# The last block's routing in a transformer-and-experts kernel: merged VectorE operations, and four weight splits postponed

## The chip, the cores and the metric

One NeuronCore of one Trainium2 chip runs the whole program. The metric is the device time of one execution in microseconds. The kernel before took 767.72, 769.78 and 770.45 us in three runs; the median is 769.78 us.

## The reference, cut to what matters

Three stages run one after the other on 2304 tokens (4 sequences of 576) of width 512, all in float32:

```
attn   = softmax(mask(q k^T / 8)) v           # 8 heads of 64, causal window of 64
h      = x @ w_in                             # 512 -> 2048
x1     = (max(h,0) + alpha*min(h,0)) @ w_out  # 2048 -> 512
logits = x1 @ w_gate                          # 8 experts
e      = argmax(logits);  p = softmax(logits)[e]
out    = p * (max(x1 @ w1[e], 0) @ w2[e])     # 512 -> 1024 -> 512, each token by its one expert
```

What the change touches is the third stage: the routing, that is which token goes to which expert, and the order in which the experts' weights are prepared.

## The kernel before, in words

**Blocks.** The 18 token tiles of 128 are cut into five blocks of 4, 4, 4, 3 and 3 tiles. Attention and the dense stage run block by block under a written-out plan, the last block (index 4, called L in the code) from line 1014 on in a loop that the framework schedules. Products are made from a high and a low part of each operand: three TensorE matmuls (hi*hi, hi*lo, lo*hi) for one exact one.

**Slots.** The expert stage works in slots: a slot is up to 128 tokens of one expert. It gathers its tokens' rows of x1 from DRAM (`gather`), transposes them (`xtr`), multiplies by w1 in four parts (`e1`), transposes the result (`htr`), multiplies by w2 in four parts (`e2mm`) and scatters the rows to the output (`finish`). Slots 0 to 7 use tokens of the first four blocks only; their table (which expert and which list column a slot has) is built in the last dense block. The other slots need the last block's routing, which is done while slots 3 to 6 run. 21 slots run with these inputs (0 to 20); slots 20 to 24 stand under a branch.

**Weights.** A slot's weights are eight pieces of 128x1024. ScalarE writes each piece's high part (`split2_hi`, line 937) and VectorE its low part (`split2_lo`, line 943) into a ring of 12 tiles. SyncE reloads the raw piece pair for a later slot behind each second split, if that slot has another expert. In `slot(s)` there are eight steps, one behind each part of the matmul work; in the kernel before step i of slot s splits piece i of slot s+1, so a piece is ready a whole slot before it is used.

**Routing of the last block.** Its logits are made in slots 0 to 2. Then two chains of small VectorE operations, `route_main` (argmax, ranks, list) and `route_side` (softmax weight, slot table), are fed in by `tick(n)`, which advances the first chain that is not held by n operations; behind each split stand up to two. HOLD makes a chain wait for the next `safe()` point. `r_rank` counts on TensorE how many earlier tokens chose each expert; `r_place` turns ranks to list positions; `r_onehot` and `r_list` write the token list `lst` by matmul; `slot_table` makes the slots' experts (`ctl`), change flags and list columns (`col`). `table_count` copies the totals by one more matmul into a bank of PSUM, out of three banks in rotation (`pbank("att")`) that `htr` and `xtr` use as well, and `ni` (line 649) reads it.

Of the kernel before, what the change touches and what calls it, by code (L numbers as in the profile page):

```python
# [21 lines left out]
LO_POOL = ()  # L22
# [58 lines left out]
def attn_moe_moe_kernel(  # L81
# [73 lines left out]
    def prep_consts():  # L155
        DVE.memset(lst, BIG)
        DVE.memset(ohsum, 0.0)
# [322 lines left out]
    def r_pick(j):  # L480
# [23 lines left out]
        yield  # L504
# [42 lines left out]
    def r_place(j):  # L547
# [8 lines left out]
        DVE.tensor_tensor(out=rr, in0=rk, in1=oh, op=ALU.mult)  # L556
        give(("R", j))
        yield
        for u in range(n):
            DVE.tensor_tensor(out=ohsum, in0=ohsum, in1=oh[:, u, :], op=ALU.add)  # L560
            yield
# [5 lines left out]
        yield  # L567
        ri = small("ri", [], I32)
        DVE.tensor_copy(out=ri, in_=rf)
# [10 lines left out]
        jf = small("jf", [])  # L580
        DVE.tensor_copy(out=jf, in_=ji)
        yield
        cf = small("cf", [])
        DVE.tensor_scalar(out=cf, in0=mx, scalar1=-float(NTILE), scalar2=float(NE * NTILE), op0=ALU.mult, op1=ALU.add)
        yield
        DVE.tensor_tensor(out=cf, in0=cf, in1=jf, op=ALU.add)
        yield
        rc[j] = (cf, pf)

    def r_onehot(j, h=0):  # L590
# [3 lines left out]
        for t in range(2 * h, min(2 * h + 2, n)):  # L594
            a = rp.tile([128, NCOL], FP32R, tag="A", bufs=2, name="A")
            bm = rp.tile([128, 128], FP32R, tag="B", bufs=2, name="B")
# [4 lines left out]
            yield  # L601
            ab[j].append((t, a, bm))
# [30 lines left out]
    def table_count(part=1):  # L633
        b = pbank("att") if part else aslot(("R", NB))
        PE.matmul(out=b[:, 0:NE], lhsT=one16, rhs=ohsum, start=True, stop=True)
        return b

    def slot_table(part):
        ns, s0 = (K1, 0) if part == 0 else (NSLOT - K1, K1)

        def small(nm, shape, dt=FP32):
            n = {"cmp": ns * NE, "es": ns, "jn": ns}.get(nm)
            pad = {} if n is None else {"padded_shape": [128, NSLOT] if len(shape) == 1 else [128, NSLOT, NE]}
            own = nm if nm in ("ni", "t8", "cmp", "es", "jn") else f"{nm}{part}"
            return e2.tile([128] + shape, dt, bufs=1, tag=own, name=nm, **pad)

        b = counted[0] if part else table_count(0)
        ni = small("ni", [NE], I32)
        DVE.tensor_scalar(out=ni, in0=b[:, 0:NE], scalar1=127.0 * part, scalar2=None, op0=ALU.add)
        yield  # L650
# [3 lines left out]
        DVE.tensor_copy(out=nb, in_=ni)  # L654
        yield
        give(("R", NB))
        if part:
            DVE.tensor_tensor(out=nb, in0=nb, in1=tab["done"], op=ALU.subtract)
            yield
# [3 lines left out]
        cum = small("cum", [NE])  # L663
        DVE.tensor_reduce(out=cum, in_=t8, axis=AX.X, op=ALU.add)
# [8 lines left out]
        ec = small("ec", [ns])  # L673
        DVE.tensor_scalar(out=ec, in0=es, scalar1=float(NE - 1), scalar2=None, op0=ALU.min)
        yield
        ctl = small("ctl", [2, ns], I32)
        DVE.tensor_copy(out=ctl[:, 0, :], in_=ec)
        yield
        DVE.tensor_tensor(out=ctl[:, 1, 1:ns], in0=ec[:, 1:ns], in1=ec[:, 0:ns - 1], op=ALU.not_equal)
        yield  # L680
        if part:
            DVE.tensor_tensor(out=ctl[:, 1, 0:1], in0=ec[:, 0:1], in1=tab["last"], op=ALU.not_equal)
            yield
            tot = small("tot", [1], I32)
# [9 lines left out]
        DVE.tensor_tensor(out=jn, in0=siota[:, 0:ns], in1=jn, op=ALU.subtract)  # L694
        yield
        col = small("col", [ns])
        DVE.scalar_tensor_tensor(out=col, in0=es, scalar=float(NTILE), in1=jn, op0=ALU.mult, op1=ALU.add)
        yield
        if part:
            DVE.tensor_tensor(out=cmp, in0=es.unsqueeze(2).to_broadcast([128, ns, NE]),  # L700
                              in1=siota[:, 0:NE].unsqueeze(1).to_broadcast([128, ns, NE]), op=ALU.is_equal)
            yield
            DVE.tensor_tensor(out=cmp, in0=cmp, in1=tab["done"].unsqueeze(1).to_broadcast([128, ns, NE]), op=ALU.mult)
            yield
            DVE.tensor_reduce(out=jn, in_=cmp, axis=AX.X, op=ALU.add)
            yield
            DVE.tensor_tensor(out=col, in0=col, in1=jn, op=ALU.add)
            yield
        else:
            done = small("done", [NE])  # L710
            DVE.tensor_tensor(out=done, in0=nb, in1=cum, op=ALU.subtract)
            yield
            DVE.tensor_scalar(out=done, in0=done, scalar1=float(K1), scalar2=0.0, op0=ALU.add, op1=ALU.max)
            yield
            DVE.tensor_tensor(out=done, in0=done, in1=nb, op=ALU.min)
            yield
            tab["done"] = done
# [10 lines left out]
    def route_main():  # L728
# [272 lines left out]
    at(last + 9, 6, lambda: drain(slot_table(0)))  # L1001
    at(last + 9, 6, sregs, 0)
# [25 lines left out]

    def slot(s):
# [147 lines left out]
```

## Time and profile before

| what | value |
| --- | --- |
| runs | 767.72, 769.78, 770.45 us |
| profiled execution, its own time | 767.73 us |
| its span, first to last instruction | 766.0 us |
| TensorE (PE) busy | 747.6 us, 98% |
| VectorE (DVE) busy | 607.0 us, 79% |
| ScalarE (ACT) busy | 455.4 us, 59% |
| mean granted TensorE clock | 0.996 |

The span is the time between the first and the last instruction; the execution's own time is 1.73 us more. Shares of busy time are averages over stages with different limits, so the expert stage is read slot by slot. A slot begins with its first matmul of line 833. Those starts are at 528.42 us for slot 3, 541.07 for slot 4, 558.92 for slot 5, 572.14 for slot 6, 585.85 for slot 7 and 598.16 for slot 8; from there on a slot follows every 12.3 us.

### The profile page before, as it was taken

The numbers are of one execution on the slowest core, as the hardware profiler recorded it, in microseconds if no ns is written. First come the engines' busy times: TensorE is split into PE (matmuls) and PEld (weight loads), VectorE is DVE, ScalarE is ACT, GpSimd is POOL, SyncE is SP. The second block draws the span as 40 slices with busy tenths as digits, with TensorE's granted clock in tenths as the row PEclk, the third lists the DMA queues.
The fourth block names the chain that finished last, engine by engine and source line by source line (L and its number), as shares of the span: only waits on it lengthen the run. The fifth ranks groups of instructions, "written<-read, shape, count | busy, mean of one in ns | idle before, by whom it ended". The sixth has DMA issues, their size and how long they took to land.

```text
span 766.0 us, 12642 instructions
## 1 busy us (share of the span) xinstructions
PE 747.6 (98%) x4572; PEld 612.7 (80%) x4572; DVE 607.0 (79%) x1149; ACT 455.4 (59%) x865; POOL 86.3 (11%) x106
## 2 busy tenths in 40 slices
PE   7999999999999999999999999999899999999996
PEld 3688888888888888888888988788677888888884
DVE  4999998477565756578875946689989999999997
ACT  4877555543233342334343224788678898899986
POOL 1210001000000000000000001021111213131322
PEclk9999999999999999999999999999999999999999
DMA  9983413133122222222223117411216776767611
GB/s 344 411 367 131 175 66 118 49 104 104 47 72 97 62 83 77 73 87 99 84 66 111 56 43 298 169 43 42 70 31 245 276 272 262 286 223 258 212 75 51
DMA packets 29442, 109.90 MB, mean 143 GB/s; under 512 B 3582, under 2 KB 3966, under 8 KB 22208
## 3 DMA queue, kind: packets, MB, share of 16 engines
q1 hardware_dynamic: 25856, 98.25, 35.6%
q0 software_dynamic: 3520, 10.80, 4.3%
q8 instruction: 38, 0.62, 0.3%
q14 instruction: 28, 0.23, 0.1%
HBM read 154.09 MB, written 10.26 MB: 215 GB/s over the span
## 4 chain that ended last, share of the span: by engine, by line
PE 90%; DVE 5%; DMA 2%; ACT 1%; issue 1%; SPq 0%; DVEq 0%; ACTq 0%
PE acc L861 14%; PE h L385 9%; PE acc L427 9%; PE h L386 8%; PE h L387 8%; PE acc L428 8%; PE acc L429 8%; PE h L835 4%; PE h L833 4%; PE h L834 4%; DVE hl L943 3%; PE att L360 3%; PE att L291 2%; PE att L337 2%; PE att L844 1%
## 5 line engine op out<-in xcount | busy, mean ns | idle before, releaser
L943 DVE TENSOR_TENSOR hl<-hl,hl 128x1024 fp32r<-128x1024 f32 x176 | 212.0, 1222 | 19.4 <-ACT hl L937 18.7
L937 ACT CAST hl<-hl 128x1024 fp32r<-128x1024 f32 x176 | 180.6, 1050 | 5.1 <-DMA hl<-in_wx_dram 4.0
L861 PE MATMUL acc<-hl,xl 128*128 128x512 f32 x504 | 132.4, 404 | 1.2 <-DVE xl L848 1.2
L400 ACT ACTIVATE g<-h 128x512 f32<-128x512 f32 (+1 forms) x80 | 44.6, 558 | 142.3 <-PE h L387 112.0
L385 PE MATMUL h<-xh,hl 128*128 128x512 f32 (+1 forms) x320 | 120.7, 377 | 0.6 <-DVE g L404 0.6
L386 PE MATMUL h<-xl,hl 128*128 128x512 f32 (+1 forms) x320 | 118.2, 369 | 0.0
L387 PE MATMUL h<-xh,hl 128*128 128x512 f32 (+1 forms) x320 | 118.1, 369 | 0.0
L428 PE MATMUL acc<-hl,gl 128*128 128x512 f32 x288 | 113.1, 393 | 0.3 <-DVE gl L410 0.3
L429 PE MATMUL acc<-hl,gh 128*128 128x512 f32 x288 | 112.7, 391 | 0.0
L427 PE MATMUL acc<-hl,gh 128*128 128x512 f32 x288 | 110.0, 400 | 0.0
L861 PEld LDWEIGHTS acc<-hl,xl 128*128 128x128 f32 x504 | 92.3, 191 | 20.9 <-DVE xl L848 3.0
L404 DVE SCALAR_TENSOR_TENSOR g<-g,beta,h 128x512 f32<-128x512 f32 (+1 forms) x80 | 55.3, 691 | 56.5 <-ACT g L400 56.3
L410 DVE TENSOR_TENSOR gl<-g,gh 128x512 fp32r<-128x512 f32 (+1 forms) x80 | 50.8, 635 | 35.7 <-PE acc L428 21.6
L345 ACT CAST gh<-g 128x512 fp32r<-128x512 f32 (+1 forms) x80 | 46.5, 582 | 51.5 <-DVE g L404 49.7
L809 POOL DMA_INDIRECT gx<-x1d,ixg x23 | 38.1, 1655 | 289.7 <-DVE xh L821 146.7
L385 PEld LDWEIGHTS h<-xh,hl 128*128 128x128 f32 x320 | 60.1, 188 | 10.7 <-issue 1.2
L833 PE MATMUL h<-hl,xh 128*128 128x512 f32 x168 | 67.9, 404 | 0.0
L477 DVE SCALAR_TENSOR_TENSOR dot<-stage,wge 128x512 bf16<-128x512 f32 x96 | 65.9, 686 | 2.0 <-DMA wge<-in_wgt_dram 0.7
L386 PEld LDWEIGHTS h<-xl,hl 128*128 128x128 f32 x320 | 60.2, 188 | 8.5 <-DVE xl L373 0.5
L387 PEld LDWEIGHTS h<-xh,hl 128*128 128x128 f32 x320 | 60.1, 188 | 7.9
L835 PE MATMUL h<-hl,xh 128*128 128x512 f32 x168 | 66.0, 393 | 0.0
L834 PE MATMUL h<-hl,xh 128*128 128x512 f32 x168 | 65.5, 390 | 0.0
(188 smaller groups left out, 1062.2 us busy)
## 6 DMA issues: line engine op xcount, KB each, us to landing
hl<-in_wx_dram SPq DMA_DIRECT2D x92, 1024.0 KB
hl<-in_wcat_dram SPq DMA_DIRECT2D x14, 1024.0 KB
qk<-in_qkv_dram SPq DMA_DIRECT2D x30, 448.0 KB
v<-in_qkv_dram SPq DMA_DIRECT2D x30, 256.0 KB
wge<-in_wgt_dram SPq DMA_DIRECT2D x24, 256.0 KB
x1d<-stage SPq DMA_DIRECT2D x3, 1032.0 KB
hl<-in_qkv_dram SPq DMA_DIRECT2D x6, 448.0 KB
x<-in_wcat_dram SPq DMA_DIRECT2D x2, 1024.0 KB
```

The costliest lines, as they stand in the source:

```text
L385: PE.matmul(out=h[:, 0:n], lhsT=w_in_op(f, k, 0), rhs=xh[:, k, :], start=(k == 0), stop=False)
L386: PE.matmul(out=h[:, 0:n], lhsT=w_in_op(f, k, 0), rhs=xl[:, k, :], start=False, stop=False)
L387: PE.matmul(out=h[:, 0:n], lhsT=w_in_op(f, k, 1), rhs=xh[:, k, :], start=False, stop=(k == 3))
L427: PE.matmul(out=a, lhsT=gh[:, c0:c0 + 128], rhs=w_out_op(f, 0), start=(f == 0), stop=False)
L428: PE.matmul(out=a, lhsT=gl[:, c0:c0 + 128], rhs=w_out_op(f, 0), start=False, stop=False)
L429: PE.matmul(out=a, lhsT=gh[:, c0:c0 + 128], rhs=w_out_op(f, 1), start=False, stop=(f == 15))
L833: PE.matmul(out=o, lhsT=th[:, k, :], rhs=wh, start=(k == 0), stop=False)
L834: PE.matmul(out=o, lhsT=th[:, k, :], rhs=wl, start=False, stop=False)
L835: PE.matmul(out=o, lhsT=tl[:, k, :], rhs=wh, start=False, stop=(k == 3))
L861: PE.matmul(out=o, lhsT=x[:, f % 4, :], rhs=w[:, lo, (f % 2) * 512:(f % 2) * 512 + 512], start=(x is th and f == 0 and lo == 0), stop=(x i ...
L937: ACT.copy(out=t[:, 0, :], in_=r)
L943: eng.tensor_tensor(out=t[:, 1, :], in0=r, in1=f32(t[:, 0, :]), op=ALU.subtract)
```

## The change

**Ranks.** The counter `ohsum` starts at 144 (8 x 18) and not at 0, so the rank matmuls give the list column's offset by themselves. `r_rank` issues one wide matmul for each earlier tile instead of one for each pair of tiles. For the last block it makes one more group of eight columns: the totals, which `table_blocks` reads beside the ranks, so `table_count` is gone.

**Place and table.** Reductions write int32 directly, two-step sums become one `scalar_tensor_tensor`, the three additions to `ohsum` are left out for the last block, the list is written once (`r_onehot(j, None)`, one `r_list`, one `r_add`), and the slot table's column comes from fewer operations. Part of the first table's work (`table_rest`) goes two iterations later in the last dense block. The softmax weight and the write of the last block's rows of x1 to DRAM stand last.

**Order.** The pieces of slots 1 to 24 are one queue, and `feed` takes the next. A table TICKS says how many routing operations go behind each step; where it says 5, the step splits nothing. That is so at step 4 of slot 2 and step 0 of slots 3, 4 and 5, so from slot 5 on step i of slot s splits the piece that came four steps earlier before: pieces 4 to 7 of the running slot in steps 0 to 3, pieces 0 to 3 of the next in steps 4 to 7.

```diff
@@ r_rank
-        for t in range(n):
-            PE.matmul(out=rk[:, t, :], lhsT=one16, rhs=ohsum, start=True, stop=False)
-            for u in range(t):
-                PE.matmul(out=rk[:, t, :], lhsT=one16, rhs=oh[:, u, :], start=False, stop=False)
-            PE.matmul(out=rk[:, t, :], lhsT=ut16, rhs=oh[:, t, :], start=False, stop=True)
+        m = n + (j == NB - 1)
+        rk = b[:, 0:m * NE].rearrange("p (t e) -> p t e", t=m)
+        PE.matmul(out=rk, lhsT=one16, rhs=ohsum.unsqueeze(1).to_broadcast([128, m, NE]), start=True, stop=False)
+        for u in range(m - 1):
+            PE.matmul(out=rk[:, u + 1:m, :], lhsT=one16, rhs=oh[:, u:u + 1, :].to_broadcast([128, m - 1 - u, NE]),
+                      start=False, stop=False)
+        PE.matmul(out=rk[:, 0:n, :], lhsT=ut16, rhs=oh, start=False, stop=True)
@@ r_place
+        if j == NB - 1:
+            table_blocks(1, rk[:, n, :])
+        else:
+            for u in range(n):
+                DVE.tensor_tensor(out=ohsum, in0=ohsum, in1=oh[:, u, :], op=ALU.add)
...
-        if j == NB - 1:
-            yield HOLD
-            counted.append(table_count())
-        rf = small("rf", [])
-        DVE.tensor_reduce(out=rf, in_=rr, axis=AX.X, op=ALU.add)
-        ri = small("ri", [], I32)
-        DVE.tensor_copy(out=ri, in_=rf)
+        ri = small("ri", [], I32)
+            DVE.tensor_reduce(out=ri, in_=rr, axis=AX.X, op=ALU.add)
...
-        DVE.tensor_copy(out=jf, in_=ji)
-        DVE.tensor_scalar(out=cf, in0=mx, scalar1=-float(NTILE), scalar2=float(NE * NTILE), op0=ALU.mult, op1=ALU.add)
-        DVE.tensor_tensor(out=cf, in0=cf, in1=jf, op=ALU.add)
+        DVE.scalar_tensor_tensor(out=cf, in0=mx, scalar=-float(NTILE), in1=ji, op0=ALU.mult, op1=ALU.add)
@@ slot_table(1): the operations that go
-        DVE.tensor_copy(out=nb, in_=ni)
-        DVE.tensor_copy(out=ctl[:, 0, :], in_=ec)
-            DVE.tensor_tensor(out=ctl[:, 1, 0:1], in0=ec[:, 0:1], in1=tab["last"], op=ALU.not_equal)
-            DVE.tensor_copy(out=tot, in_=cum[:, NE - 1:NE])
-        DVE.tensor_tensor(out=jn, in0=siota[:, 0:ns], in1=jn, op=ALU.subtract)
-            DVE.tensor_tensor(out=cmp, in0=es.unsqueeze(2).to_broadcast([128, ns, NE]),
-                              in1=siota[:, 0:NE].unsqueeze(1).to_broadcast([128, ns, NE]), op=ALU.is_equal)
-            DVE.tensor_tensor(out=cmp, in0=cmp, in1=tab["done"].unsqueeze(1).to_broadcast([128, ns, NE]), op=ALU.mult)
-            DVE.tensor_reduce(out=jn, in_=cmp, axis=AX.X, op=ALU.add)
-            DVE.tensor_tensor(out=col, in0=col, in1=jn, op=ALU.add)
@@ the order of the slots
+    pieces = [(s, i) for s in range(1, NSLOT) for i in range(8)]
+    def feed(n=1):
+            s, i = pieces.pop(0)
+            split2(s, i)
+            if i % 2 and s + 1 < NSLOT:
+                if i == 1:
+                    sregs(s + 1)
+                reload(s + 1, i // 2)
+    TICKS = """
...
+00005000
+51110110
...
-                split2(s + 1, i)
-                if not early or i > 5:
-                    tick(2)
-                if i % 2 and s + 2 < NSLOT:
-                    if i == 1:
-                        sregs(s + 2)
-                    reload(s + 2, i // 2)
+            n = int(ticks.get(i, 0))
+            if n < 5:
+                feed()
+            tick(n)
```

VectorE, kernel before, from the logits of the last tile (`lg`, in slot 2) on: `m`, `eq`, `mx` and `oh` are the argmax, `ls` is the softmax's first step, rows of line 943 are the splits' low parts.

```order
L459 COPY lg<-att_68 128x8
L943 TENSOR_TENSOR hl_4918<-hl_4694,hl_4918 128x1024
L488 TENSOR_REDUCE m<-lg 128x3
L492 TENSOR_TENSOR eq<-lg,m 128x24
L943 TENSOR_TENSOR hl_4924<-hl_4694,hl_4924 128x1024
L494 TENSOR_TENSOR eq<-eq,c 128x24
L497 TENSOR_REDUCE mx<-eq 128x3
L943 TENSOR_TENSOR hl_4967<-hl_4688,hl_4967 128x1024
L500 TENSOR_TENSOR oh<-eq,mx 128x24
L943 TENSOR_TENSOR hl_4977<-hl_4688,hl_4977 128x1024
L513 TENSOR_TENSOR ls<-lg,m 128x24
```

VectorE, changed kernel, the same place (splits are line 934 there, the transposed tokens' low part `xh` line 813).

```order
L458 COPY lg<-att_68 128x8
L487 TENSOR_REDUCE m<-lg 128x3
L491 TENSOR_TENSOR eq<-lg,m 128x24
L493 TENSOR_TENSOR eq<-eq,c 128x24
L496 TENSOR_REDUCE mx<-eq 128x3
L499 TENSOR_TENSOR oh<-eq,mx 128x24
L794 SCALAR_TENSOR_TENSOR scr,ixf<-c,col,lst 128x152
L798 TENSOR_SCALAR ixg<-ixf 128x1
L799 CAST ixs<-ixf 128x1
L813 TENSOR_TENSOR xh<-att_67,xh 128x512
L934 TENSOR_TENSOR hl_4872<-hl_4637,hl_4872 128x1024
```

The five argmax operations stood between four splits and now stand together in the place of one split, in slot 2.

VectorE, kernel before, in slot 4: the read of the totals (`ni`, line 649) stands behind a split, a list operand and a gather, and right in front of `xh`, the read of the bank (acc_5006) that slot 5's tokens are transposed into.

```order
L943 TENSOR_TENSOR hl_4967<-hl_4692,hl_4967 128x1024
L600 TENSOR_SCALAR B<-c,pf 128x128
L802 SCALAR_TENSOR_TENSOR scr,ixf<-c,col,lst 128x152
L806 TENSOR_SCALAR ixg<-ixf 128x1
L807 CAST ixs<-ixf 128x1
L649 TENSOR_SCALAR ni<-acc_5006 128x8
L821 TENSOR_TENSOR xh<-acc_5006,xh 128x512
```

VectorE, changed kernel: the totals (`ni`, line 638) are read with the ranks (`rr`), at step 0 of slot 3.

```order
L934 TENSOR_TENSOR hl_4869<-hl_4639,hl_4869 128x1024
L555 TENSOR_TENSOR rr<-att_68,oh 128x24
L638 TENSOR_SCALAR ni<-att_68 128x8
L565 TENSOR_REDUCE ri<-rr 128x3
L568 TENSOR_SCALAR pi<-ri 128x3
L571 TENSOR_SCALAR ji<-ri 128x3
L574 CAST pf<-pi 128x3
L577 SCALAR_TENSOR_TENSOR cf<-mx,ji 128x3
L934 TENSOR_TENSOR hl_4875<-hl_4639,hl_4875 128x1024
L590 TENSOR_SCALAR A<-c,cf 128x152
```

Both are now read a slot earlier, out of one bank, and the bank's next writer (slot 4's tokens) comes three transposes later.

TensorE, changed kernel, ranks of a block of four tiles (14 matmuls of 8 columns before).

```order
L537 LDWEIGHTS c_70
L537 MATMUL att_68<-ohsum,c_70 128x32
L539 LDWEIGHTS c_70
L539 MATMUL att_68<-oh,c_70 128x24
L539 LDWEIGHTS c_70
L539 MATMUL att_68<-oh,c_70 128x16
L539 LDWEIGHTS c_70
L539 MATMUL att_68<-oh,c_70 128x8
L541 LDWEIGHTS c_70
L541 MATMUL att_68<-oh,c_70 128x32
```

Nine matmuls and their weight loads are gone from each such block.

## Rows read from the trace of the kernel before

**Rows 1.** The page, first part: busy time, share of the span, instructions.

```profile
PE 747.6 (98%) x4572; PEld 612.7 (80%) x4572; DVE 607.0 (79%) x1149; ACT 455.4 (59%) x865; POOL 86.3 (11%) x106
```

**Rows 2.** Windows: length, busy PE, PEld, DVE, ACT, POOL, clock, DMA; slots 3 to 7.

```profile
528.42:541.07 12.65, 12.65 (x70) 10.26 (x69) 12.38 (x27) 11.21 (x15) 2.62 (x3) 1.00 0.14 44
541.07:550.75 9.68, 9.68 (x46) 7.22 (x44) 9.58 (x20) 8.44 (x11) 2.88 (x2) 1.00 0.39 137
550.75:554.09 3.34, 0.01 (x2) 0.01 (x1) 3.25 (x12) 0.18 (x1) 0.00 (x0) 1.00 0.00 0
554.09:558.92 4.83, 4.83 (x17) 3.88 (x17) 3.23 (x6) 2.48 (x3) 0.97 (x1) 0.65 0.22 55
558.92:572.14 13.22, 12.92 (x65) 10.45 (x63) 11.60 (x30) 11.09 (x14) 1.02 (x1) 1.00 0.06 21
572.14:585.85 13.71, 12.84 (x61) 10.03 (x60) 13.55 (x23) 11.10 (x14) 2.32 (x3) 1.00 0.51 168
585.85:598.16 12.31, 12.31 (x61) 10.18 (x60) 11.77 (x16) 11.12 (x14) 2.93 (x3) 1.00 0.92 355
```

**Rows 3.** Waits, 480 to 766 us: who for whom, total, times, longest.

```profile
PE acc L817 <- DVE ni L649: 3.3, 1, 3.3
```

**Rows 4.** Timeline of PE, slot 4: start, length, instruction.

```profile
554.50 4.58 PE L861 MATMUL acc<-hl,xl 128*128 128x512 f32 x12
```

**Rows 5.** Chain that ended last, slot 8: start, length, instruction.

```profile
602.41 0.44 PE acc L844 x4
604.24 1.39 PE acc L861 x6
607.89 2.77 PE acc L861 x12
```

**Rows 6.** Timeline of DVE, slot 8.

```profile
603.85 0.68 DVE L848 TENSOR_TENSOR xl<-acc,xl 128x512 fp32r<-128x512 f32 x1
...
607.67 1.23 DVE L943 TENSOR_TENSOR hl<-hl,hl 128x1024 fp32r<-128x1024 f32 x1
...
609.35 0.68 DVE L821 TENSOR_TENSOR xh<-att,xh 128x512 fp32r<-128x512 f32 x1
609.95 1.22 DVE L943 TENSOR_TENSOR hl<-hl,hl 128x1024 fp32r<-128x1024 f32 x1
```

**Rows 7.** Timeline, slots 3 to 5: small operations of the routing on DVE.

```profile
530.28 0.17 DVE L488 TENSOR_REDUCE m<-lg 128x3 f32<-128x24 f32 x1
530.48 0.18 DVE L492 TENSOR_TENSOR eq<-lg,m 128x24 f32<-128x24 f32 x1
530.58 1.22 DVE L943 TENSOR_TENSOR hl<-hl,hl 128x1024 fp32r<-128x1024 f32 x1
...
547.32 0.16 DVE L575 TENSOR_SCALAR ji<-ri 128x3 int32<-128x3 int32 x1
547.39 0.16 DVE L578 CAST pf<-pi 128x3 f32<-128x3 int32 x1
...
550.67 0.35 DVE L597 TENSOR_SCALAR A<-c,cf 128x152 fp32r<-128x152 f32 x1
550.94 0.28 DVE L600 TENSOR_SCALAR B<-c,pf 128x128 fp32r<-128x128 f32 x1
...
565.34 0.29 DVE L671 TENSOR_REDUCE es<-cmp 128x17 f32<-128x136 f32 x1
```

**Rows 8.** Timeline of PE: ranks of the first block, and the list.

```profile
233.53 0.18 PE L539 MATMUL att<-ohsum,c 128*128 128x8 bf16 x1
...
233.90 0.48 PE L427 MATMUL acc<-hl,gh 128*128 128x512 f32 x1
...
560.29 0.34 PE L611 MATMUL att<-A,B 128*128 128x152 f32 x2
```

**Rows 9.** The page, fifth part: the last dense block's one wait for DVE.

```profile
L385 PE MATMUL h<-xh,hl 128*128 128x512 f32 (+1 forms) x320 | 120.7, 377 | 0.6 <-DVE g L404 0.6
```

**Rows 10.** Reads of x1 in DRAM: from issue to landing, least, median, most.

```profile
DMA to landing us min/median/max: 3.3/4.9/8.4
```

More of the change, by code (lines that the diff above doesn't have):

```diff
@@ L156, in prep_consts @@
         DVE.memset(lst, BIG)
-        DVE.memset(ohsum, 0.0)
+        DVE.memset(ohsum, float(NE * NTILE))
     def hl_tile(s, dt, n):
@@ L555, in r_place @@
         rr = small("rr", [NE])
[L556 removed]
+        DVE.tensor_tensor(out=rr, in0=rk[:, 0:n, :], in1=oh, op=ALU.mult)
+        if j == NB - 1:
[3 more added lines that the diff above has]
+                DVE.tensor_tensor(out=ohsum, in0=ohsum, in1=oh[:, u, :], op=ALU.add)
         give(("R", j))
         yield
[L559 to L567 removed]
         ri = small("ri", [], I32)
[L569 removed]
+        with nc.allow_low_precision(reason="whole numbers under 2**24"):
+            DVE.tensor_reduce(out=ri, in_=rr, axis=AX.X, op=ALU.add)
         yield
@@ L631, in attn_moe_moe_kernel, with tsmall @@
     e2 = None
[L633 to L639, printed above, removed]
+    def tsmall(part):
+        ns = K1 if part == 0 else NSLOT - K1
         def small(nm, shape, dt=FP32):
@@ L643, in small, with table_blocks, slot_table @@
             pad = {} if n is None else {"padded_shape": [128, NSLOT] if len(shape) == 1 else [128, NSLOT, NE]}
-            own = nm if nm in ("ni", "t8", "cmp", "es", "jn") else f"{nm}{part}"
+            own = nm if nm in ("t8", "cmp", "es", "jn") else f"{nm}{part}"
             return e2.tile([128] + shape, dt, bufs=1, tag=own, name=nm, **pad)
-        b = counted[0] if part else table_count(0)
+        return ns, small
+    def table_blocks(part, cnt):
+        ns, small = tsmall(part)
         ni = small("ni", [NE], I32)
-        DVE.tensor_scalar(out=ni, in0=b[:, 0:NE], scalar1=127.0 * part, scalar2=None, op0=ALU.add)
-        yield
+        DVE.tensor_scalar(out=ni, in0=cnt, scalar1=127.0 * part - 128.0 * NE * NTILE, scalar2=None, op0=ALU.add)
+        tab["ni", part] = ni
+    def slot_table(part):
+        ns, small = tsmall(part)
+        if part == 0:
+            b = aslot(("R", NB))
+            PE.matmul(out=b[:, 0:NE], lhsT=one16, rhs=ohsum, start=True, stop=True)
+            table_blocks(0, b[:, 0:NE])
+            give(("R", NB))
+        ni = tab["ni", part]
         DVE.tensor_scalar(out=ni, in0=ni, scalar1=7, scalar2=None, op0=ALU.logical_shift_right)
@@ L653, in slot_table @@
         nb = small("nb", [NE])
-        DVE.tensor_copy(out=nb, in_=ni)
+        if part:
+            DVE.tensor_tensor(out=nb, in0=ni, in1=tab["done"][:, 0:NE], op=ALU.subtract)
+        else:
+            DVE.tensor_copy(out=nb, in_=ni)
         yield
[L656 to L659, printed above, removed]
         t8 = small("t8", [NE, NE])
@@ L662, in slot_table @@
         yield
-        cum = small("cum", [NE])
-        DVE.tensor_reduce(out=cum, in_=t8, axis=AX.X, op=ALU.add)
+        cum = small("cum", [NE], I32)
+        with nc.allow_low_precision(reason="whole numbers up to 25"):
+            DVE.tensor_reduce(out=cum, in_=t8, axis=AX.X, op=ALU.add)
         yield
@@ L1001, in attn_moe_moe_kernel @@
     at(last + 9, 6, lambda: drain(slot_table(0)))
+    at(last + 11, 6, table_rest)
     at(last + 9, 6, sregs, 0)
@@ L1026, in attn_moe_moe_kernel @@
         run_fill(it)
+    pieces = [(s, i) for s in range(1, NSLOT) for i in range(8)]
+    def feed(n=1):
+        for _ in range(n):
+            if not pieces:
+                return
+            s, i = pieces.pop(0)
[5 more added lines that the diff above has]
+    TICKS = """
+00000000
+00000000
+00005000
+51110110
+51110111
+51110111
+11110111
+"""
     def slot(s):
@@ L1057, in slot @@
         mark()
-        tick(1)
         step(2)
```

124 lines of the change are left out of this document (59 added, 65 removed).

## The prediction

> **What bounds the kernel now.** I read the page first: TensorE is busy for 98% of the span, VectorE for 79% [rows 1]. These are averages, so the expert stage comes next, in windows cut at each slot's first matmul [rows 2]. Slot 7 takes 12.31 us. TensorE is busy throughout it, VectorE for 11.77 us. That is the floor of a slot. Slots 3 to 6 take 12.65, 17.85 (9.68 + 3.34 + 4.83), 13.22 and 13.71 us, 57.43 in all, against 4 x 12.31 = 49.24. So 8.2 us are lost there, and these are the slots in which the last block's routing runs.
>
> The reason is in the VectorE column. It adds up to 12.38 + 9.58 + 3.25 + 3.23 + 11.60 + 13.55 = 53.59 us busy in those four slots, against 4 x 11.77 = 47.08 without routing: 50 small operations cost 6.5 us, 0.13 each, where only 4 x 0.54 = 2.2 us were free. VectorE works in order. What TensorE waits for (low parts of transposed tokens, reads that free a bank) stands behind splits and small operations.
>
> The waits show the worst place: `xtr` of slot 5 waits 3.3 us for `ni` [rows 3]. VectorE is busy in 3.25 of those 3.34 us [rows 2], so it is late, not idle. Then TensorE pays again: its granted clock falls from 1.00 to a mean of 0.65 in the next 4.83 us, and the twelve matmuls of `e2mm` take 4.58 us there against 2.77 in slot 8 [rows 2, 4, 5]. So about 1.8 of the 8.2 us are clock, and 3.3 the wait itself.
>
> **The change part by part.**
>
> *Routing on VectorE.* By the two orders, 50 operations become 35, five of them in slot 2, 30 in slots 3 to 5, none in slot 6. Their price goes by the rows [rows 7]. A dependent operation starts 0.20 us after its source (530.28 to 530.48), an independent one 0.07 (547.32 to 547.39), a split 0.10 behind the last one (530.48 to 530.58), the operand A costs 0.27; for B I take 0.2, and for an operation over 136 elements 0.3 (one lasts 0.29). Then:
> - place group, step 0 of slot 3 (rr, ni, ri, pi, ji, pf, cf): 1.0 us
> - table group, step 0 of slot 4 (B, ni, nb, t8, cum): 0.95
> - column group, step 0 of slot 5 (dd, cmp, jn, col, ls): 1.0
> - three A and two B: 1.2; cmp, es, ec, lst, ch: 1.1; gs twice and the reciprocal: 0.4
>
> The sum is 5.6 us. Forms that the trace does not show (a reduction into int32, int32 inputs of a scalar_tensor_tensor) are taken as their nearest float rows. All 30 at 0.07 would be 2.1 us, all at 0.35 10.5; I stay at 5.6, because each group is built from a row of its own kind.
>
> In the row, `pf` starts 0.07 us behind `ji`, which lasts 0.16 [rows 7]. The Trainium skill, VectorE: DVE Perf Modes, section The DRAIN you can't avoid, says that a VectorE operation does not start before the pipe of the one in front is empty; here the row differs. By the rule each of the 30 would cost its whole length (0.16 to 0.35 in those rows, some 6.8 us in all), and the result would be 1.2 us later, still inside the forecast's own range.
>
> *Postponed splits.* One split less in each of slots 2, 3, 4 and 5. A split takes 1.22 [rows 6]; I take 1.2 with its neighbour. In slots 3 to 6 that is 3 x 1.2 = 3.6 us. VectorE then has 47.1 + 5.6 - 3.6 = 49.1 us of work there, where 53.6 stood, against a TensorE floor of about 50 (below). It fits, barely. The argmax group of slot 2 takes 0.9 us in the place of a 1.2 us split, so slot 3 does not start later for VectorE.
>
> The price is lead. From slot 5 on a piece is ready half a slot later. I compare slot 8's times [rows 5, 6], slot start 598.16, next 610.47. Three parts of `e1` end at 602.41, so one takes 1.4 us. The split of step 4 (607.67 to 608.90) becomes piece 0 of slot 9, needed at 610.47: 1.6 us to spare. Step 5 (609.95 to 611.17) becomes piece 1, needed at 611.9: 0.7. The other six have 1.0 or more by the same pitch. Nothing waits in a settled slot, so this costs 0. Each reload still has seven steps between its issue and its split: SyncE's queue is shifted, not shortened, and the ring's older tiles are free earlier than before.
>
> *Read of the totals.* `ni` now stands beside `rr` at the start of slot 3. The bank goes back to TensorE a slot before it is wanted, so the 3.34 us wait and the clock behind it go together. What is late next is VectorE's own queue: in slots 3 and 4 the low part behind `htr`. In slot 8 it lasts from 603.85 to 604.53 and is needed by the fifth of six matmuls from 604.24, 604.24 + 4 x 0.23 = 605.16: 0.6 us to spare. With a 1.0 us group in the split's place and one A or cmp (0.3) in front, it comes about 0.4 to 0.6 later. I put 0.5 us for both slots together (bounds 0 and 2).
>
> *TensorE.* Slot 3 keeps its 12.65 (fewer rank matmuls against one wider group). Slot 4 gets all three list matmuls; two last 0.34 [rows 8], so I add 0.3. Floor: 12.65 + 12.6 + 2 x 12.31 = 49.9, with the 0.5 50.4. **Slots 3 to 6: 57.4 - 50.4 = 7.0 us less.**
>
> *Ranks of the first four blocks.* 14 matmuls take 233.53 to 233.90, 0.37 us, 0.026 each [rows 8]. Five remain: at the same pitch 0.13, so 0.24 less in three blocks and 0.13 in the fourth, **0.85 us**, because TensorE has no cover there (it bounds the dense stage; in all of it the busiest line waits 0.6 us for VectorE [rows 9]). The remaining matmuls have up to 32 columns, which no row shows; at the pace of the list's 152 columns (0.17) five would cost 0.85 and the block lose 0.5. Range of the term: -0.85 to +2; I take the first, since 32 columns are nearer to 8.
>
> *The last dense block's order.* Its loop is placed by a scheduler, and a dozen dense matmuls and the first table's operations stand some places earlier or later. Nothing is removed there that TensorE waited for, apart from the 0.6 us [rows 9]. I take 0, bounds -1 and +1.
>
> *Moved DMA.* The write of the last block's rows of x1 goes from slot 4 to the start of slot 6, on SyncE behind a reload, in front of the next. Its first reader is the gather of slot 8, issued behind step 4 of slot 6, some 8 us later; GpSimd has only gathers and scatters behind it, and those tokens are transposed a further slot later. Indirect reads land in 3.3 to 8.4 us [rows 10]; if the write took as long, it would still be covered. Cost 0; without that cover up to 2 us.
>
> Sum: -7.0 - 0.85 = -7.9. The profiled execution took 767.73, so 759.9 by it. It is the fastest of three runs, 2.05 us under the median of 769.78; taken from the median, 761.9.
>
> **The rivals.**
>
> *The groups hold TensorE up.* Five dependent operations behind each other are a block of 1 us in an in-order queue. If in slots 3, 4 and 5 something in front (a ScalarE cast) keeps VectorE back as well, each low part is 1 us late. For it: slot 6 loses 1.4 us without any single long wait [rows 2]. Against it: the group takes the place of a 1.2 us split. Price 3 to 4 us: 765 to 766.
>
> *Weights arrive late in every slot.* This is the one that ends slower. Piece 1 has 0.7 us to spare in slot 8. If the shorter lead makes VectorE's splits later against TensorE by d, each of the 14 slots from 7 to 20 waits d - 0.7. The gain is gone at d = 0.7 + 7.9/14 = 1.26 us, and it is slower by over 0.5% from 1.54 us on; at 2 us it is 780. For it: VectorE is busy for 11.77 of 12.31 us. Against it: the order and number of operations in a settled slot do not change, so nothing makes it later.
>
> *It isn't the routing.* If slots 3 to 6 were slow because of ScalarE or the reloads, the change would return little: 768. For it: DMA is busy at 0.51 in slot 6. Against it: it is busier at 0.92 in slot 7, which takes 12.31 [rows 2].
>
> *More than the sum.* If the scheduler's new order also closes waits in the last block, up to 2 us more: 760.
>
> **How the numbers follow.** The forecast has 0.72, with its own range 759.5 to 764.5. The groups' rival has 0.12, late weights 0.06, no effect 0.05, more than the sum 0.05. A measurement tells 0.5% (3.85 us) from no change, so faster means under 765.9. Forecast and more give 0.77, and most of the groups' rival 0.10: faster 0.87. Its rest and the no-effect case give 0.07 for no difference. Late weights give 0.06 for slower. The range goes from 758.5 to 766, the groups' rival at its worst, because the runs themselves differ by 2.7 us.
>
> **What would show it.** After the change the first matmuls of slots 3 to 7 should stand about 12.7, 12.8, 12.4 and 12.3 us apart, with no wait of `xtr` for `ni`, the granted clock at 1.00 in all four, and VectorE busy for about 49 us. Slots 7 to 20 should stay at 12.31; any slot over 12.5 there proves late weights. Rank groups in the first blocks should span 0.13 us. I am wrong if slots 3 to 5 show waits of TensorE for a low part of 1 us each, or if slots 3 to 6 are at 50 us and the total has still not moved by 6.

## The result, and the profile after

The changed kernel takes 761.4 us (median of 4 runs, 760.54 to 762.52) against 768.9 us (4 runs) for the kernel before beside it: a ratio of 0.9902, 95% interval 0.9877 to 0.9926. A second series gave 761.42 us (4 runs) and 0.9896, interval 0.9881 to 0.9911. The forecast was 761.9 us. The profiled execution has a span of 759.7 us, before 766.0.

The page's first part, changed kernel; it answers to [rows 1].

```profile
PE 744.7 (98%) x4530; PEld 611.7 (81%) x4535; DVE 599.7 (79%) x1119; ACT 452.4 (60%) x861; POOL 90.3 (12%) x106
```

The shares are within one point of those before. Nothing in them tells that 1% of the time is gone; the windows do. These are slots 3 to 7 of the changed kernel (columns as in [rows 2]).

```profile
528.60:541.14 12.54, 12.54 (x66) 10.16 (x65) 11.22 (x25) 10.16 (x13) 2.27 (x2) 1.00 0.14 43
541.14:553.88 12.74, 12.74 (x65) 10.46 (x64) 12.60 (x25) 10.17 (x13) 3.33 (x3) 1.00 0.14 43
553.88:566.18 12.30, 12.30 (x62) 10.18 (x61) 11.76 (x22) 10.27 (x14) 2.89 (x3) 1.00 0.13 43
566.18:578.48 12.30, 12.30 (x62) 10.19 (x61) 11.90 (x19) 11.12 (x14) 4.15 (x3) 1.00 0.32 109
578.48:590.79 12.31, 12.31 (x62) 10.18 (x60) 11.68 (x16) 11.11 (x14) 2.89 (x3) 1.00 0.87 335
```

Slots 3 to 6 take 49.88 us where they took 57.43: 7.55 us less. TensorE is busy for all of it, its granted clock is 1.00 in each slot, and VectorE has 47.48 us of work where it had 53.59. Of TensorE's waits in the expert stage, which were led by `xtr` for `ni` [rows 3], one is left, in slot 0. The second matmul group of `e2mm` in slot 4, 4.58 us long before [rows 4], takes 3.02 us, as it does in slot 8 of the kernel before in the same view.

```profile
PE acc L836 <- ACT hr L830: 0.4, 1, 0.4
```

```profile
551.02 3.02 PE L853 MATMUL acc<-hl,xl 128*128 128x512 f32 x12
```

The ranks of the first block, on TensorE: 234.79 to 234.93, 0.14 us where 14 matmuls took 0.37 [rows 8].

```profile
234.79 0.19 PE L537 MATMUL att<-ohsum,c 128*128 128x32 bf16 x1
234.82 0.22 PE L539 MATMUL att<-oh,c 128*128 128x24 bf16 x3
234.90 0.18 PE L541 MATMUL att<-oh,c 128*128 128x32 bf16 x1
234.93 0.47 PE L426 MATMUL acc<-hl,gh 128*128 128x512 f32 x1
```

Two differences lie outside these slots. The first is ahead of them. Executions differ by up to 1.7 us in when the first block's ranks start, whatever the kernel, so time is counted from there. To the start of slot 1 it takes 266.5 us with the merged routing (mean of 7 profiles, 266.3 to 266.7; the two of the lighter first slot, experiments 9 and 10, stand apart) and 267.7 without it (5 profiles, 267.5 to 267.9): 1.2 us less. The first matmul of slot 0 is no good as a mark. Behind it stand six dense matmuls more than before, 0.23 us apart, so the stages ahead look shorter by them and slot 0 longer (18.16 us against 17.54). These are the windows of slot 0, before and after:

```profile
483.58:501.12 17.54, 16.77 (x83) 12.73 (x81) 12.84 (x18) 13.72 (x19) 0.86 (x1) 1.00 0.33 121
483.19:501.35 18.16, 17.69 (x89) 14.00 (x87) 13.64 (x19) 14.78 (x21) 0.84 (x1) 1.00 0.31 116
```

The second is the end: the span ends 21.15 us after the last slot's start, before 20.08, and GpSimd's last scatter lasts 2.01 us there.

```profile
753.00 2.01 POOL L860 DMA_INDIRECT out_dram<-gx,ixs  x1 [0.30 <-ACTq L1105]
```

Together: -1.2 - 7.55 + 1.07 = -7.7 us, against 7.5 and 8.3 us between the medians of the two series. The two profiled spans differ by 6.3 us only, mostly because in this pair the changed kernel's first ranks start 1.26 us later.

### The profile page after: what moved, and what is told of

The parts are those of the page before. It is cut to its first block, busy times and chain, and to the rows that moved or that the text cites. A ratio compares the mean times of both kernels' runs of the same rounds, so it can differ in the third digit from the quotient of the medians.

```text
span 759.7 us, 12517 instructions
## 1 busy us (share of the span) xinstructions
PE 744.7 (98%) x4530; PEld 611.7 (81%) x4535; DVE 599.7 (79%) x1119; ACT 452.4 (60%) x861; POOL 90.3 (12%) x106
## 4 chain that ended last, share of the span: by engine, by line
PE 89%; DMA 4%; ACT 2%; DVE 2%; issue 1%; SPq 0%; POOL 0%; POOLq 0%
PE acc L853 14%; PE acc L426 9%; PE h L384 9%; PE h L385 8%; PE h L386 8%; PE acc L427 8%; PE acc L428 8%; PE h L825 5%; PE h L827 5%; PE h L826 5%; PE att L359 2%; PE att L836 2%; DMA gx<-x1d,ixg 2%; PE att L290 2%; PE att L336 2%; DMA hl<-in_wcat_dram 1%
## 5 line engine op out<-in xcount | busy, mean ns | idle before, releaser
L934 DVE TENSOR_TENSOR hl<-hl,hl 128x1024 fp32r<-128x1024 f32 x172 | 207.4, 1222 | 21.0 <-ACT hl L929 20.1
L929 ACT CAST hl<-hl 128x1024 fp32r<-128x1024 f32 x172 | 176.8, 1049 | 4.2 <-DMA hl<-in_wx_dram 3.3
L853 PE MATMUL acc<-hl,xl 128*128 128x512 f32 x504 | 130.0, 400 | 0.0
L801 POOL DMA_INDIRECT gx<-x1d,ixg x23 | 39.9, 1735 | 283.9 <-DVE xh L813 173.9
```

The source lines that it names most:

```text
L853: PE.matmul(out=o, lhsT=x[:, f % 4, :], rhs=w[:, lo, (f % 2) * 512:(f % 2) * 512 + 512], start=(x is th and f == 0 and lo == 0), stop=(x i ...
L929: ACT.copy(out=t[:, 0, :], in_=r)
L934: DVE.tensor_tensor(out=t[:, 1, :], in0=r, in1=f32(t[:, 0, :]), op=ALU.subtract)
```

## The experiments

Every run stood beside runs of the kernel before on its chip (medians 768.9 to 769.7 us). "Slots 3 to 6" is the time from the first matmul of slot 3 to that of slot 7, from the profile; it settles more than the medians, whose runs spread over 2 to 3 us.

**1. Own bank.** The kernel before, with only the totals moved.

```diff
-        b = pbank("att") if part else aslot(("R", NB))
+        b = bank("acc2", 1) if part else aslot(("R", NB))
```

> The kernel before with one edit: the totals that ni reads go to the eighth PSUM bank (acc2), which the expert stage leaves unused, so no transpose of tokens has to wait for that read. Theory 'sum of work' (VectorE has 53.6 us of work in slots 3 to 6 and TensorE's floor there is 49.9, every operation in front counts): the wait for ni goes, but the low part behind it stands in the same late queue, so slots 3 to 6 still take 54 to 56 us of the 57.4, and the whole run is 1.5 to 3.5 us shorter than the kernel before. Rival 'one wait' (the 3.3 us wait for ni and the 1.8 us of half clock behind it are a loss of their own): 5.1 us go, slots 3 to 6 take 52.3 us.

Measured: 765.64 us (5 runs), ratio 0.9953, interval 0.9937 to 0.997; slots 3 to 6 take 54.08 us. Slot 5's window (columns as in [rows 2]), and the waits of the expert stage (total, times, longest):

```profile
554.52:569.50 14.98, 13.21 (x65) 10.38 (x63) 14.77 (x37) 11.10 (x14) 3.12 (x2) 1.00 0.11 36
```

```profile
PE acc L861 <- DVE xl L848: 2.4, 2, 1.5
```

Slot 4 goes from 17.85 to 12.76 us: 5.09 us, the 3.34 of the wait and 1.75 of the low clock, the 1.8 that the prediction had read for it. But slot 5 rises from 13.22 to 14.98, and TensorE now waits 1.5 us for `xl` there, where it waited 0.3; the other wait of that row is slot 6's, 0.87 as before. VectorE had used the long wait to catch up; without it the same backlog shows a slot later. The run is 3.9 us shorter, a little over the 1.5 to 3.5 forecast.

**2. Only postponed.** The kernel before with its 50 routing operations, and the queue of pieces (`feed`) of the changed one, so that the same four splits are postponed.

```diff
-                split2(s + 1, i)
+            if (s, i) not in {(2, 4), (3, 0), (4, 0), (5, 0)}:
+                feed()
```

> The kernel before with its 50 routing operations and its ticks, with the same four splits postponed (step 4 of slot 2, step 0 of slots 3, 4 and 5) and all later pieces four steps later. Theory 'sum of work': 53.6 - 3 x 1.15 = 50.1 us of VectorE work in slots 3 to 6 against the floor of 49.9, so 51 to 53 us there and a run of 1 to 3 us over the changed kernel, most of the gain without any merging. Rival 'one wait': ni is still read behind the gather of slot 4, the wait of 3.3 us and its half clock stay, slots 3 to 6 take 55 us or more.

Measured: 768.55 us (10 runs), ratio 0.9988, interval 0.9973 to 1.0003; slots 3 to 6 take 56.46 us, 0.97 less than before. Slot 4's window, VectorE ahead of `ni` (start, length), TensorE's wait, and `ni` in the kernel before:

```profile
542.22:559.66 17.44, 14.25 (x63) 11.19 (x61) 15.11 (x35) 10.14 (x13) 3.86 (x3) 0.90 0.26 91
```

```profile
546.92 1.22 DVE L943 TENSOR_TENSOR hl<-hl,hl 128x1024 fp32r<-128x1024 f32 x1 [0.50 <-ACT hl L937]
...
552.74 1.22 DVE L943 TENSOR_TENSOR hl<-hl,hl 128x1024 fp32r<-128x1024 f32 x1
554.62 0.16 DVE L649 TENSOR_SCALAR ni<-acc 128x8 int32<-128x8 f32 x1
```

```profile
554.83 0.66 PE L817 MATMUL acc<-c,gx 128*128 128x128 f32 x4 [3.19 <-DVE ni L649]
```

```profile
553.88 0.15 DVE L649 TENSOR_SCALAR ni<-acc 128x8 int32<-128x8 f32 x1
```

Slot 4 has one split less, and the wait is still 3.19 us. At 546.92 VectorE had been idle for 0.50 us, waiting for a cast of ScalarE. Of the split's 1.2 us only 0.41 reached `ni`: it starts 12.40 us into the slot, before 12.81 (553.88 less 541.07). TensorE came for the bank 0.27 us sooner too, so the wait shrank by 0.14. The wait is set by the place of `ni`, behind the split of step 4, `B` and the gather's list, while TensorE wants the bank before all of these.

**3. Both edits, no merging.** The kernel before with the edits of experiments 1 and 2.

> The kernel before with both edits of the first two experiments and no merging: all 50 routing operations stay, the totals have their own PSUM bank, and the four splits are postponed. Theory 'two limits' (the place where ni is read costs 5 us of wait and half clock, the sum of VectorE's work costs some 4, and each hides the other): with both gone the work is about 50.3 us against a floor of 49.9, so slots 3 to 6 take 50.3 to 51.5 us (54.1 and 56.5 with one edit alone) and the run is at most 1.5 us over the changed kernel. Rival 'merging is needed' (chains of dependent small operations hold TensorE up by themselves): slots 3 to 6 stay over 53 us.

Measured: 764.31 us (5 runs), ratio 0.9937, interval 0.9914 to 0.9961; slots 3 to 6 take 52.45 us (12.56, 12.44, 13.76 and 13.69; the last two are shown):

```profile
554.26:568.02 13.76, 13.17 (x64) 10.38 (x63) 13.55 (x35) 10.16 (x13) 3.11 (x2) 1.00 0.13 39
568.02:581.71 13.69, 12.92 (x62) 9.82 (x60) 13.54 (x23) 11.09 (x14) 2.31 (x3) 1.00 0.11 38
```

Neither number was met. The work adds up to 50.0 us, about what was expected, but it isn't spread evenly, and a slot with room does not give it to the next: slots 3 and 4 stay at TensorE's floor with 11.10 and 11.77 us of VectorE work, slots 5 and 6 take VectorE's 13.55 us and 0.15 to 0.2 more. So the theory was restated slot by slot, and the next run tests it.

**4. Both edits, splits left out elsewhere.** As experiment 3, with other steps that split nothing.

```diff
-    SKIP = {(2, 4), (3, 0), (4, 0), (5, 0)}
+    SKIP = {(2, 4), (5, 0), (5, 4), (6, 0)}
```

> The same kernel as with both edits of before and no merging, but the four splits are left out at step 4 of slot 2, steps 0 and 4 of slot 5 and step 0 of slot 6. The sum of VectorE's work in slots 3 to 6 stays 50 us; only its spread changes, from 11.1, 11.8, 13.6, 13.5 us to about 12.4, 12.6, 12.4, 12.3 (from the run with the own bank alone: 12.38, 12.62, 14.77, 13.54, less 1.2 for each split). Theory 'slot by slot' (a slot takes the larger of TensorE's 12.3 and VectorE's work of that slot plus 0.15): 12.6, 12.75, 12.5, 12.5, that is 50.2 to 50.8 in all, and the run is 1.5 to 2.5 us faster than with the skips at slots 3 to 5 (764.3), so beside the changed kernel without any merging. Rival 'only the sum counts': 52.0 to 52.9 as before, 764.

Measured: 763.51 us (5 runs), ratio 0.9915, interval 0.9902 to 0.9929; slots 3 to 6 take 51.47 us (12.56, 12.78, 13.83 and 12.30; the last two are shown), between the two forecasts:

```profile
555.80:569.63 13.83, 13.16 (x65) 10.37 (x63) 13.62 (x36) 9.20 (x12) 3.86 (x3) 1.00 0.12 39
569.63:581.93 12.30, 12.30 (x62) 10.19 (x60) 11.45 (x21) 10.15 (x13) 2.21 (x3) 1.00 0.13 43
```

The rule holds, the spread put into it did not: slot 5 still got 13.62 us of work, slot 6 only 11.45. A slot's work is read from the same trace as its length, so the rule describes a run better than it forecasts one. The sum hardly moved (49.8 us) while the time fell by 0.98, so it isn't the sum that counts. Without merging, two placements stay 1.6 and 2.6 us over the changed kernel's 49.88; a better one was not tried.

**5. Nothing postponed.** The changed kernel, every step splits.

```diff
-            if n < 5:
-                feed()
+            feed()
```

> The changed kernel with its merged routing and its order of routing operations, but no split postponed: each step splits one piece, also the four that hold a group of five. Theory 'sum of work': VectorE has 47.5 + 3 x 1.15 = 50.9 us of work in slots 3 to 6 and one split more in slot 2, over TensorE's floor of 49.9, and the lead of a whole slot does not help, because what TensorE waits for stands behind the splits: slots 3 to 6 take 51 to 53 us (49.9 in the changed kernel), the run is 1.5 to 3.5 us longer than the changed kernel. Rival 'one wait': there is no wait for ni, so it takes what the changed kernel takes.

Measured: 762.32 us (4 runs), ratio 0.9907, interval 0.9888 to 0.9927; slots 3 to 6 take 52.41 us. Slots 3 and 4:

```profile
527.98:541.45 13.47, 13.12 (x67) 10.08 (x65) 13.40 (x27) 11.10 (x14) 3.90 (x2) 1.00 0.13 40
541.45:555.31 13.86, 12.92 (x65) 10.47 (x63) 13.72 (x26) 11.11 (x14) 3.34 (x3) 1.00 0.12 40
```

Postponing is worth 2.5 us in these slots. The medians show 0.9 of it, short of the 1.5 to 3.5 forecast, since this kernel's last scatter takes 1.02 us and its last slot 19.79, 1.4 less than the changed kernel's.

**6. One split fewer postponed, and one more.** The changed kernel, `if n < 5 or s == 5`, and `if n < 5 and (s, i) != (6, 0)`.

> The changed kernel with three splits postponed: step 0 of slot 5 splits a piece as well as its group of five. Theory 'sum of work': slot 5 has 11.8 + 1.15 = 12.9 us of VectorE work and takes 12.7 to 13.2 us (12.30 in the changed kernel), nothing else changes, the run takes 761.8 to 762.5. Rival 'lead' (a longer lead is worth something by itself in later slots): under 761.4.

Measured with three: 760.62 us (4 runs), ratio 0.9894, interval 0.9863 to 0.9925. Slot 5:

```profile
553.14:565.90 12.76, 12.56 (x61) 10.10 (x60) 12.65 (x23) 11.22 (x15) 2.93 (x3) 1.00 0.13 41
```

The slot does what "sum of work" said. The whole run is under its range: here too the last scatter takes 1.02 us. By its number (under 761.4) the rival is met, but it has no slot to show for itself: slots 7 to 19 are the same to 0.03 us.

> The changed kernel with a fifth split postponed (step 0 of slot 6), so that from slot 7 on each piece comes one step later still. By the prediction's margins step 5's split ends 0.7 us into the next slot, and it would now be piece 0, needed at its start. Theory 'four is the limit': each of the 14 slots from 7 to 20 waits 0.7 to 0.9 us, 13.0 to 13.2 us each, the run takes 771 to 774 us. Rival 'VectorE moves ahead' (it is idle for 0.6 us a slot and uses that): under 0.3 us a slot, under 766 us.

Measured with five: 770.34 us (10 runs), ratio 1.0021, interval 1.0007 to 1.0034. A settled slot, its wait, and the waits of the stage:

```profile
577.36:590.31 12.95, 12.61 (x61) 10.10 (x60) 11.69 (x16) 11.11 (x14) 2.90 (x3) 1.00 0.83 292
```

```profile
655.21 0.39 PE L825 MATMUL h<-hl,xh 128*128 128x512 f32 x1
655.93 0.50 PE L826 MATMUL h<-hl,xh 128*128 128x512 f32 x1 [0.33 <-DVE hl L934]
```

```profile
PE h L826 <- DVE hl L934: 4.9, 14, 0.4
```

Each of the slots from 7 on takes about 12.96 us, 0.65 more, a little under the forecast. The waits of the row, 0.35 each, are counted from the modelled end of a matmul. From start to start the second matmul comes 0.72 us behind the first, where it is 0.23 otherwise, so 0.49 of the 0.65 is lost there. VectorE did not move ahead, though it has idle time in every slot. This is the prediction's slower rival: one step less of lead gives back everything. The changed kernel's own margin agrees. Its split of step 4 in slot 8 ends at 601.52. Its next starts at 602.58 and, at 1.22 us, ends at 603.80; the next slot begins at 603.13. As piece 0 that second one would be 0.67 late for the slot's start, 0.44 for the second matmul, the first to read a low part. As piece 1, needed 1.4 us on, it has the 0.7 to spare that was read from [rows 5, 6].

```profile
600.29 1.23 DVE L934 TENSOR_TENSOR hl<-hl,hl 128x1024 fp32r<-128x1024 f32 x1
...
602.58 2.35 DVE L934 TENSOR_TENSOR hl<-hl,hl 128x1024 fp32r<-128x1024 f32 x2
```

```profile
603.13 0.39 PE L825 MATMUL h<-hl,xh 128*128 128x512 f32 x1
```

**7. No groups.** The changed kernel with the same four splits left out, but its operations fed two at a time.

```diff
-51110110
-51110111
+22222222
+22222222
...
-            if n < 5:
+            if (s, i) not in {(2, 4), (3, 0), (4, 0), (5, 0)}:
```

> The changed kernel with the same four postponed splits, but the routing operations two at a time behind nearly every step and not in groups of five. Same operations in the same order. Theory 'sum of work': only the sum counts, slots 3 to 6 within 0.6 us of the changed kernel's 49.9, the run within 1 us of it. Rival 'place of the group' (five operations stand exactly where a split is missing, and the low parts come in time only so): 2 us or more longer.

Measured: 761.12 us (4 runs), ratio 0.9892, interval 0.9866 to 0.9917; slots 3 to 6 take 50.04 us, 0.16 more, and TensorE has no wait of over 0.2 us in them. Grouping is neither the gain nor a danger.

**8. Half a split more in ten slots.** The changed kernel, and behind step 4:

```diff
+            if i == 4 and 8 <= s <= 17:
+                t = ring[s + 1, 0]
+                DVE.tensor_tensor(out=t[:, 1, 0:512], in0=raw2[0][:, 0:512], in1=f32(t[:, 0, 0:512]), op=ALU.subtract)
```

> The changed kernel, and in each of slots 8 to 17 VectorE writes half of the piece of step 4 a second time (128x512, the same values, some 0.65 us). Nothing else is added. VectorE's work in these slots rises from 11.75 to about 12.4 us. Theory 'slot by slot' (VectorE's work plus 0.15 where that is over TensorE's 12.3): 12.5 to 12.6 us each, the run 2 to 3 us over the changed kernel. Rival 'the free 0.5 us is not at this place' (the low part of the next tokens stands right behind): 12.8 to 12.95 each, 5 to 6.5 us more. Third: nothing, under 0.5 us more, if VectorE's busy time is not what holds a slot.

Measured: 762.01 us (4 runs, 760.09 to 763.41), ratio 0.9894, interval 0.9879 to 0.9909, 0.6 over the changed kernel beside it, with runs that overlap. Two of the ten slots, one as eight of them are and one of the two others:

```profile
666.21:678.57 12.36, 12.36 (x62) 10.07 (x61) 12.21 (x17) 11.27 (x15) 3.90 (x2) 1.00 0.99 383
...
641.03:653.87 12.84, 12.65 (x61) 10.06 (x60) 12.69 (x19) 11.32 (x15) 3.90 (x2) 1.00 0.28 103
```

```profile
628.30 1.05 ACT L929 CAST hl<-hl 128x1024 fp32r<-128x1024 f32 x1 [0.95 <-DMA hl<-in_wx_dram]
...
638.69 1.23 DVE L934 TENSOR_TENSOR hl<-hl,hl 128x1024 fp32r<-128x1024 f32 x1 [0.45 <-ACT hl L929]
...
641.84 0.50 PE L827 MATMUL h<-hl,xh 128*128 128x512 f32 x1 [0.19 <-DVE xh L813]
```

The forecast of 2 to 3 us failed. VectorE's busy time rose by 0.5 us in most of these slots, to 12.2 and not to 12.4, and the eight slots lost about 0.05 each. "Work plus 0.15" gives 12.35 for 12.2, so there the rule stands and its input was wrong; the third theory's bound of 0.5 us is missed by less than the runs differ, and this run doesn't separate the two. It shows that a settled slot has room for one more operation of 0.6 us at this place. Slots 11 and 12, which lost 0.35 and 0.50, are another matter: ScalarE waits 0.95, 0.16 and 0.39 us for reloaded weights in slot 11, VectorE 0.45 for the cast behind the last of them, and TensorE 0.19 for `xh` as slot 12 begins. Slot 11 takes 12.66 us with 11.95 of VectorE work, which the rule doesn't cover. Why those reloads landed late is open.

**9. A lighter first slot.** The changed kernel with two splits of slot 0 done in slots 1 and 2 instead.

```diff
-            if n < 5:
-                feed()
+            if n < 5 and (s, i) not in {(0, 0), (0, 1)}:
+                feed(2 if (s, i) in {(1, 5), (2, 6)} else 1)
```

> The changed kernel with two splits taken out of steps 0 and 1 of slot 0 and done as a second split in slots 1 and 2, where VectorE has 1.6 us free per slot. In the changed kernel slot 0 takes 18.2 us, and two casts of splits stand on its chain between the copies of the dense result and the first relu. Theory 'ScalarE's queue holds slot 0': it takes 16.2 to 17.2 us, slots 1 and 2 stay at 13.6, the run takes 759.5 to 760.5. Rival 'TensorE's own order sets slot 0': 18 us as before, 761.4.

Measured: 760.11 us (4 runs), ratio 0.9883, interval 0.9852 to 0.9914. Slot 0 takes 17.40 us, not 16.2 to 17.2. The chain of slot 0 (start, length, what), first of the changed kernel, then of this one:

```profile
487.62 0.95 ACT stage L434 x2
...
489.06 1.07 ACT hl L929
490.13 0.49 ACT g L448
490.61 0.95 ACT hl L929
491.56 0.51 ACT hr L830
...
492.11 0.66 PE acc L836 x4
```

```profile
488.47 0.44 PE att L446 x4
488.91 0.23 PE h L825
...
491.66 0.44 PE acc L836 x4
```

The two casts (`hl`, line 929) are gone from the chain, and it stays on TensorE, which then bounds the slot at 17.4. So ScalarE's queue did hold slot 0 of the changed kernel, for 0.7 us, and behind it was the next limit that the range had not allowed for.

**10. Changed kernel and lighter first slot, once more side by side.**

> The changed kernel once more, unchanged, for the end of the run: in its profile the last scatter took 2.01 us and the last slot 21.15 us, in most other kernels 1.02 and some 20. If that belongs to the program, it is there again, and the median is 761 to 762; if it belongs to one execution, the scatter takes 1.02 and the span is about 758.7.

> The kernel with the lighter first slot again, in five rounds beside the changed kernel. Slot 0 took 17.40 us against 18.16. If that is what it is worth, the median is 0.5 to 1.5 us under the changed kernel's of this call; if the first reading was chance, under 0.3 us.

Measured: 761.42 us (761.1 to 762.28) for the changed kernel, and 759.68 us (758.26 to 759.99, 4 runs, ratio to the kernel before 0.9868, interval 0.9853 to 0.9883) for the lighter first slot, the fastest of this study: 1.7 us less, with no run in common. That is over the 0.5 to 1.5 forecast. Slot 0 gives 0.70 of it (18.14 and 17.44 us) and the last slot 0.64 (21.13 and 20.49); slots 1 to 19 are the same to 0.10 us in all. The long scatter is there again in the changed kernel, so it belongs to the program; in the other kernel it takes 1.02 us.

```profile
753.22 2.01 POOL L860 DMA_INDIRECT out_dram<-gx,ixs  x1 [0.30 <-ACTq L1105]
```

```profile
751.50 1.02 POOL L860 DMA_INDIRECT out_dram<-gx,ixs  x1 [0.30 <-ACTq L1105]
```

## Why the prediction was right

**The place and the size.** Slots 3 to 6 were to take about 12.7, 12.8, 12.4 and 12.3 us, 50.4 by the sum; they take 12.54, 12.74, 12.30 and 12.30, 49.88. The wait for `ni` and the low clock went together, as said. Experiments 1 to 5 price the parts: own bank alone 3.35 us, postponing alone 0.97, both 4.98, the change without postponing 5.02, the whole change 7.55. The first limit hides the second. That the whole gain needs the merging is not shown: without it two placements of the splits were tried, and a better one may exist.

**A close total, in part by luck.** The slots gave 0.55 us more than forecast and the stages ahead 0.35; the end, which no term had, took 1.07 back.

**The clock: right by two views.** The prediction set the 4.58 us of a timeline, which runs to the modelled end of the last matmul, beside the 2.77 us of a chain, which doesn't. In one view the group lost 1.56 us. The 1.8 it named is right for the slot: TensorE's busy time fell by 1.76 in experiment 1.

**VectorE's work: mis-sized.** 49.1 us was forecast, 47.48 measured. Taking off 3.6 us for three splits, the 30 operations cost 47.48 - (47.08 - 3.6) = 4.0 us, 0.13 each, not 0.19. The prediction had this number: 6.5 us for 50 operations [rows 2] is 0.13. It priced each one anew by the start-to-start distance of dependent ones, but most have something independent around them. The place group shows it:

```profile
531.60 0.18 DVE L555 TENSOR_TENSOR rr<-att,oh 128x24 f32<-128x24 f32 x1
531.70 0.16 DVE L638 TENSOR_SCALAR ni<-att 128x8 int32<-128x8 f32 x1
531.81 0.18 DVE L565 TENSOR_REDUCE ri<-rr 128x3 int32<-128x24 f32 x1
532.03 0.17 DVE L568 TENSOR_SCALAR pi<-ri 128x3 int32<-128x3 int32 x1
532.11 0.16 DVE L571 TENSOR_SCALAR ji<-ri 128x3 int32<-128x3 int32 x1
532.23 0.17 DVE L574 CAST pf<-pi 128x3 f32<-128x3 int32 x1
532.31 0.15 DVE L577 SCALAR_TENSOR_TENSOR cf<-mx,ji 128x3 f32<-128x3 f32 x1
```

Seven operations take 0.86 us; `pi` waits 0.22 for `ri`, while `ji` follows it after 0.08. The rule of the Trainium skill that the prediction set beside this (VectorE: DVE Perf Modes, The DRAIN you can't avoid) would cost each its whole length, 0.15 to 0.18 here. That is half of what the section says: it adds that a next operation that is not held back starts earlier, and with that half the trace agrees, as at `ji`.

**The half us for late low parts: about nothing.** No matmul waits over 0.2 us for a low part in slots 3 to 6; one weight load waits 0.26 for `xl` in slot 4. In slot 3 VectorE has 11.22 us of work in 12.54, so it had 1.3 in hand.

**"It is late, not idle": true, and not enough.** VectorE is busy in 3.25 of the 3.34 us, and the prediction rightly gave the end of the wait to the move of `ni`. But the same row invites the reading that less work would end it, and that is false: experiment 2 took work away and the wait stayed. A busy engine in front of a late operation tells that the operation stands behind others, not that less work earlier would bring it forward.

**The ranks and the last dense block.** Five matmuls of up to 32 columns take 0.14 us (0.13 forecast), so the group of the first block gives 0.23 of the 0.24. From one block's ranks to the next block's it is 0.23 less in three blocks, as forecast. From the fourth block's ranks to slot 1 it is 0.5 less, against 0.13 and a term of 0 with bounds of 1 for the reordered block: inside the bounds, and the wait of 0.6 [rows 9] is gone there, but another of 0.5, for `gl`, has come. Slot 0 is not longer by a loss: it has six dense matmuls more, and 0.92 us more of TensorE work, for 0.62 more time.

**DMA at 0, settled slots unchanged.** Slots 7 to 19 take 12.30 to 12.34 us as before: the lead holds, by the margin that experiment 6 bounds. What no step of it had is the 1.07 us at the end.

**The rivals.** "The groups hold TensorE up" fell with experiment 7; "late weights" is real, but one step further on (experiment 6); "it isn't the routing" fell with experiments 1 and 5; "more than the sum", up to 2 us from waits closed in the last block, gave some 0.4.

## What to carry to other kernels

Count each engine's work per stage of the pipeline, not over the stages: in this kernel, where no single late read or late weight held it, a slot took the larger of TensorE's 12.3 us and VectorE's work in it plus 0.07 to 0.21 us (13.40 gave 13.47, 13.72 gave 13.86, 14.77 gave 14.98), and room in slots 3 and 4 did not help slots 5 and 6 (experiment 3). Where one long wait ends a stage, ask what lies behind it before pricing its removal, and ask of the late operation what it stands behind, not how busy its engine is. Price many small operations by the mean that the windows give for their kind, and a postponed step by its spare time against the moment of its use.

## What the runs showed of the hardware

- The cost of an idle TensorE goes on: after the 3.19 us wait of experiment 2, as after the one of before, the granted clock fell (0.90 as the mean of that slot), and removing the wait of 3.34 us in experiment 1 gave 5.09 us. Waits of up to 1.5 us, in that run, left the clock at 1.00 in slots 3 to 7.
- A bf16 matmul of 24 or 32 columns is followed by the next after some 0.03 us (234.79 to 234.82 and 234.90 to 234.93), as one of 8 columns was (14 in 0.37 us).
- VectorE starts an operation before the one in front has ended if it doesn't need its result: `ji` 0.08 us behind `pi`, which lasts 0.17; `pi`, which needs `ri`, starts 0.22 behind it.
- The last scatter takes 2.01 us in the changed kernel (both profiles) and in experiments 7 and 8, and 1.02 us in the kernel before and all other experiments. Its cause was not found.
